# Attention outputs stored by quads and read back with the 16 rows of a head outermost, in a fused attention and mixer kernel

## The chip, the cores and the metric

The kernel runs on one core of one Trainium2 chip. The metric is the device time of one execution in microseconds (us). Beside the runs there is one profiled execution, from which every row of the profile comes. Engines are named as the profile names them: PE multiplies matrices (PEld is its weight load), DVE, ACT and POOL work on tiles, and SP issues the DMA transfers; SPq is SP's queue of instructions. Lines of the profile carry L43 nearly everywhere, because every instruction is issued through one helper at line 43; the tile names tell the groups apart.

## The reference

All is float32. One input `x` of 2048 tokens by 512 channels goes through a layer norm; the result feeds two branches, and a gate joins them.

```python
xn = layernorm(x)
# A: attention, 32 heads of 16 channels, each query sees the 256 latest keys
q, k, v = split_heads(xn @ wqkv)
s = merge_heads(softmax(mask(q @ k.T * 16 ** -0.5)) @ v) @ wo
# B: a second layer norm, 512 -> 1792 -> 512
g = silu(gelu(layernorm(xn) @ w1 + b1) @ w2 + b2)
out = x + s * g
```

## The kernel before

**Stages.** Four stages follow one another on PE: the layer norm and first projections; attention; then the two-layer branch B in four chunks of 512 tokens (`c` from 0 to 3), where each chunk ends with the product of its attention outputs with `wo` and the gate (`end_chunk`, line 953). A product of two float32 operands is made from high and low parts in three passes (`PASSES`), with the split into `hi` and `lo` done by ACT and DVE.

**Attention.** The 32 heads are handled in 8 quads of four heads (`n`). A quad has 16 blocks of 128 queries (`qb`), and each block is one slot `t = 16 n + qb` of a plan written out by hand: the loop at lines 826 to 858 issues each slot's score, probability and value products and, between them, fill work, in a fixed order. `at(t, ...)` puts a step inside slot t, `behind(t, ...)` at its end. `pv_step` (line 577) gives the unnormalised outputs of one block: head j of the quad lies in partitions 32 j to 32 j + 16, sixteen output rows and, as the seventeenth, the sum of the probabilities. ACT or DVE copies them to the tile `oraw` (printed `outs[0]`), and after four blocks one DMA of 256 KB writes `oraw` to `oT_d` in memory (line 597). There are 32 such stores.

**How the outputs come back.** `oT_d` has four groups `g` of eight heads, quads 2 g and 2 g + 1. `fetch_sums` (line 881) loads all sums into `den`; DVE takes their inverses in chunk 0, at steps 4 and 5 of the chunk's loop, and one DMA writes them to `rden_d` (line 1149). `load_o` (line 916) then brings, for a chunk and a group, the 128 output rows (`raw`, in the trace `or<-oT_d`) and beside them the inverse sums, each repeated over its head's 16 rows (`rec`, in the trace `w<-rden_d`). Both are 256 KB. In both the order of partitions is head by head, with 16 rows inside. DVE multiplies them, `split_o` splits the product into `ohl`, and `end_chunk` multiplies it by `wos`, the rows of `wo` in the same order. `wo` is brought in that order by the host, copied within memory by `stage_in` (line 638) during attention, and loaded by `fetch`.

**Order around the change.** On PE, DVE, ACT and POOL the program order is kept. On SP it is kept during attention and in chunks 0 and 1 (`nc.sync.on`); elsewhere the framework orders the issues. In chunk 0, step 5 issues the write of `rden_d`, then four pairs of `raw` and `rec` loads, and then sixteen loads of 64 KB into `xnT` (`fetch_y`, line 909), four for each of four parts `kt`, with short runs of 128 bytes; these hold the transposed inputs of chunk 1. Step 12 splits part 0 (ACT makes `yh<-xnT`, DVE the low part), and step 13 starts with ACT's `gh`, which PE needs for its next product. The ACT part of that split therefore stands ahead of the last `gh` of the chunk.

Of the kernel before, what the change touches and what calls it, by code (L numbers as in the profile page):

```python
# [9 lines left out]
F32 = mybir.dt.float32  # L10
# [7 lines left out]
S, D, H, DH, WIN, F = 2048, 512, 32, 16, 256, 1792  # L18
P = 128
NCH = S // 512  # L20
# [3 lines left out]
NQ = H // 4  # L24
# [26 lines left out]
def mixer_kernel(ctx, tc, x, wqk, wv, wo, w1, b1, w2, b2, out):  # L51


    nc = SimpleNamespace(**{name: Ordered(tc, name) for name in ("tensor", "vector", "scalar", "gpsimd", "sync")})
# [5 lines left out]
    dram = ctx.enter_context(tc.tile_pool(name="dram", bufs=1, space=bass.MemoryType.DRAM))  # L60
# [16 lines left out]
    def load(pool, tag, src, name, shape=(P, 512)):  # L77
        t = pool.tile(list(shape), F32, tag=tag, name=name)
        nc.sync.dma_start(t, src)
        return t  # L80
# [95 lines left out]
    def open_slot(i):  # L176
# [3 lines left out]
    wva = bigp.tile([P, 2, KT, 256], F32R, tag="wa", name="wva")  # L180
    wqs = {}
    xn_d = dram.tile([8, P, D], F32, name="xn_d")
    oT_d = dram.tile([4, 8, 32, S], F32, name="oT_d")
    rden_d = dram.tile([4, 8, S], F32, name="rden_d")
    h_d = dram.tile([EARLY - 2, P, 512], F32, name="h_d")
    w_d = {"w1": dram.tile([P, NF * 512], F32, name="w1_d"), "w2": dram.tile([P, NF * 512], F32, name="w2_d"),
           "wo": dram.tile([P, 4 * 512], F32, name="wo_d")}
# [387 lines left out]
    outs = {}  # L575

    def pv_step(n, qb):

        lo = max(qb - 2, 0)
        for kb in range(lo, qb + 1):  # L580
            for j in range(4):
                nc.tensor.matmul(otb[32 * j: 32 * j + DH + 1], vt[:, kb, (4 * n + j) % 16],
                                 pts[n, kb, j // 2][:, j % 2, P * (qb - kb): P * (qb - kb + 1)],
                                 start=(kb == lo), stop=(kb == qb),
                                 skip_group_check=True, tile_position=(0, 32 * j))
        if qb % 4 == 0:
            outs[0] = sgp.tile([P, 512], F32, tag="or", name=f"oraw_{n}_{qb}", bufs=2)
        t = 16 * n + qb + 1
        by = nc.vector.tensor_copy if t in ends_pair else nc.scalar.copy
        outs["copy"] = by(outs[0][:, P * (qb % 4): P * (qb % 4 + 1)], otb)  # L590
        last = outs["second" if t in ends_pair else "copy"]
        old = t - 3
        if old >= 0:
            for w in writers[old // 16, old % 16, 0] + writers[old // 16, old % 16, 1]:
                tc.add_manual_dep(last.ins, w.ins.name, ORDER, reason="the next slot writes in its place")
        if qb % 4 == 3:
            (at if n or qb > 7 else behind)(16 * n + qb + 2, nc.sync.dma_start, oT_d[n // 2, n % 2::2, :, P * (qb - 3): P * (qb + 1)], outs[0])


    mlp = {}  # L600
# [37 lines left out]
    def stage_in(kind, k):  # L638

        sl = slice(1024 * k, 1024 * (k + 1))  # L640
        nc.sync.dma_start(w_d[kind][:, sl], {"w1": w1, "w2": w2, "wo": wo}[kind][:, sl])

    def fetch(kind, f):

# [66 lines left out]
    n, raw = raws["qk"]  # L711
# [60 lines left out]
    for k, (kind, j) in enumerate([*(("w1", j) for j in range(7)), *(("w2", j) for j in range(7)), ("wo", 0), ("wo", 1)]):  # L772
        behind(23 + 4 * k, stage_in, kind, j)
# [52 lines left out]
    for t in range(-16, end + 1):  # L826
# [25 lines left out]
        if t >= 1:  # L852
            pv_step((t - 1) // 16, (t - 1) % 16)
# [27 lines left out]
    def fetch_sums():  # L881
        den = t2.tile([P, 512], F32, tag="t2", name="den")
        for g in range(4):
            nc.sync.dma_start(den[32 * g: 32 * g + 32], oT_d[g, :, DH].rearrange("a (c t) -> a c t", c=NCH))
        return den

    mlp["y"] = [load(mlp["yp"], "y", xn_d[4 + i], f"y_1_{i}") for i in range(4)]
    for f in range(6, NF, 2):
        t = gp.tile([P, 2, 512], F32, tag="ohl", name=f"hr_{f}", bufs=4)
        nc.sync.dma_start(t, h_d[f - 6: f - 4].rearrange("f p t -> p f t"))  # L890
        ready.update({f: t[:, 0], f + 1: t[:, 1]})
        if f == 8:
            den = fetch_sums()
# [22 lines left out]
    def load_o(c, g):  # L916

        cols = slice(512 * c, 512 * (c + 1))
        pool, tag = (t2, "t2") if c else (mlp["yp"], "y")
        raw = load(pool, tag, oT_d[g, :, 0:DH, cols], f"or_{c}_{g}")  # L920
        rec = mlp["w2", g // 2][:, 512 * (14 + g % 2): 512 * (15 + g % 2)].bitcast(F32)
        nc.sync.dma_start(rec, bass.AP(tensor=rden_d.tensor, offset=rden_d.offset + 8 * g * S + 512 * c,
                                       ap=[[S, 8], [0, DH], [1, 512]]))
        return raw, rec

    def split_o(c, g, raw):
# [169 lines left out]
    for c in range(2):  # L1096
# [24 lines left out]
        for i in range(NF + 1):  # L1121
# [16 lines left out]
            if c == 0:  # L1138
                if i == 3:
                    mlp["ln"] = layernorm(mlp["y"], "C1", True)  # L1140
                    y_steps(0, 5)
                if i == 4:
                    y_steps(5, 10)
                    turn_y(1, range(4))
                if i in (4, 5):
                    for j in (2 * i - 8, 2 * i - 7):
                        nc.vector.reciprocal(den[:, P * j: P * (j + 1)], den[:, P * j: P * (j + 1)])
                if i == 5:
                    nc.sync.dma_start(rden_d.rearrange("g a (c t) -> (g a c) t", c=NCH), den)
                    wanted += [load_o(0, g) for g in range(4)]  # L1150
                    for kt in range(KT):
                        fetch_y(1, kt, mlp["yy"][1][kt].bitcast(F32))
                for kt in {12: (0,), 13: (1,), 14: (2, 3)}.get(i, ()):
                    split(mlp["yy"][0][kt], mlp["yy"][1][kt], mlp["yy"][1][kt].bitcast(F32))
            else:
                steps2(i)
# [5 lines left out]
            if c and 0 <= k < 4:  # L1162
                wanted.append(load_o(c, k))
# [35 lines left out]
    for g in range(NG + 1):  # L1199
        if g < NG:  # L1200
            if g + 1 < NG:
                fetch_pair(g + 1)
            if g > NG - 3:
                raws_o = [load_o(2, 2 * (g - NG + 2) + k) for k in range(2)]
# [89 lines left out]
    for i in range(NF):  # L1294
# [9 lines left out]
        if 5 <= i < 9:  # L1304
            raw, rec = wanted
# [37 lines left out]
```

## Time and profile before

| quantity | value |
|---|---|
| median of 3 runs (all runs) | 741.33 us (741.27, 741.33, 744.54) |
| profiled execution, own time | 742.66 us |
| its span, first to last instruction | 740.9 us |
| mean granted TensorE clock | 0.998 |
| PE busy | 724.8 us, 98% of the span |
| DVE, ACT, POOL busy | 509.9, 444.0, 297.8 us |
| stores `oT_d<-oraw` | 32 of 256 KB |
| loads `or<-oT_d` and `w<-rden_d` | 16 each, of 256 KB |

The profile's page gives busy times, the chain of work that ended last, and the costliest groups. Other views of the same execution are used too: busy time by stretches (with the granted clock, the busy share of the 16 DMA engines and what they moved), the instructions of one engine in order of time, and the sums of waits. Busy time of PE includes the pipelined end of each product, so PE counted as busy can still be held for a fraction of a microsecond.

### The profile page before, as it was taken

What the parts mean: (1) busy time and instruction counts of PE and PEld (TensorE: products, weight loads), DVE (VectorE), ACT (ScalarE), POOL (GpSimd) and SP (SyncE); (2) the same over time, 40 slices, a digit from 0 to 9 for tenths busy, and PEclk for the clock granted to TensorE, in tenths of its full rate; (3) what the DMA queues carried; (4) which work ended last, traced back from release to release, by engine and by line L of the source; (5) the groups of instructions that cost most, each with busy time, mean ns of one, the idle gap of its engine ahead of it and who ended that gap; (6) DMA issues with size and microseconds to landing.
All of it is one profiled execution on the core that took longest, in us unless ns stands there. A gap on an engine that the chain in (4) does not pass through costs nothing.

```text
span 740.9 us, 18755 instructions
## 1 busy us (share of the span) xinstructions
PE 724.8 (98%) x7360; PEld 586.4 (79%) x7360; DVE 509.9 (69%) x790; ACT 444.0 (60%) x744; POOL 297.8 (40%) x644
## 2 busy tenths in 40 slices
PE   8999999999999999999999999999999999999997
PEld 7886777777778888777776688788888888888886
DVE  6886676867766778887772677656667855667643
ACT  7757777877777676788877766443644734542001
POOL 7413767867666555767877600120102000001102
PEclk9999999999999999999999999999999999999999
DMA  8633355766556535647724485746453322263611
GB/s 291 193 70 78 83 142 150 193 173 191 150 142 155 145 89 143 165 115 187 206 83 156 129 288 185 186 137 203 110 109 106 106 80 79 65 184 117 213 56 57
DMA packets 84025, 105.71 MB, mean 143 GB/s; under 512 B 36640, under 2 KB 36896, under 8 KB 83936
## 3 DMA queue, kind: packets, MB, share of 16 engines
q1 hardware_dynamic: 83936, 104.50, 49.8%
q8 instruction: 58, 0.95, 0.6%
q14 instruction: 31, 0.25, 0.1%
HBM read 54.53 MB, written 32.77 MB: 118 GB/s over the span
## 4 chain that ended last, share of the span: by engine, by line
PE 86%; DMA 4%; ACT 4%; DVE 3%; SPq 1%; POOL 1%; issue 1%; DVEq 0%; ACTq 0%
PE fb L43 18%; PE acc L43 18%; PE zo L43 13%; PE p L43 9%; PE stb L43 9%; PE s L43 6%; PE h L43 6%; PE xy L43 5%; PE pv L43 3%; ACT pt L43 3%; DMA qk<-sh 1%; DMA w<-rden_d 1%; SPq L43 1%; POOL pt L43 1%; DMA qk<-qk 1%
## 5 line engine op out<-in xcount | busy, mean ns | idle before, releaser
L43 POOL TENSOR_SCALAR_AFFINE_SELECT pt<-pt 128x256 f32<-128x256 f32 x480 | 193.1, 426 | 128.8 <-ACT pt L43 124.9
L43 ACT ACTIVATE pt<-stb 128x768 f32<-128x768 f32 (+1 forms) x244 | 188.6, 773 | 52.7 <-PE stb L43 46.3
L43 DVE TENSOR_REDUCE mt<-xy 128x4 f32<-128x1024 f32 (+1 forms) x128 | 152.6, 1192 | 4.4
L43 DVE COPY_PREDICATED xy<-upper,zo 128x512 f32<-128x512 int32 x112 | 77.8, 694 | 70.3 <-PE xy L43 63.7
L43 POOL TENSOR_TENSOR xo<-xo,gated 128x512 f32<-128x512 f32 x15 | 19.9, 1330 | 237.3 <-DVE gated L43 195.5
L43 PE MATMUL fb<-xnT,wqb 64*128 64x512 f32 (+1 forms) x684 | 104.6, 397 | 0.0
L43 PE MATMUL zo<-pt,vt 128*17 128x128 f32 x2880 | 103.7, 275 | 0.3 <-POOL pt L43 0.3
L43 PE MATMUL stb<-qk 64*128 64x384 f32 (+1 forms) x488 | 94.9, 383 | 6.1 <-ACT pt L43 4.3
L43 PE MATMUL acc<-w,gh 128*128 128x512 f32 x320 | 98.6, 389 | 0.7 <-ACT gh L43 0.7
L43 PEld LDWEIGHTS stb<-qk 64*128 64x128 f32 x488 | 45.9, 183 | 48.4 <-ACT pt L43 41.6
L43 PEld LDWEIGHTS zo<-pt,vt 128*17 128x17 f32 x2880 | 67.5, 97 | 15.7 <-issue 5.0
L43 PEld LDWEIGHTS fb<-xnT,wqb 64*128 64x128 f32 (+1 forms) x684 | 64.9, 185 | 9.3 <-issue 0.6
L43 PEld LDWEIGHTS acc<-w,gh 128*128 128x128 f32 x320 | 60.0, 188 | 13.5 <-ACT gh L43 1.2
L43 PE MATMUL acc<-w,gl 128*128 128x512 f32 x160 | 62.4, 390 | 1.0 <-DVE gl L43 1.0
L43 PE MATMUL xy<-qk 64*128 64x256 f32 (+2 forms) x536 | 58.4, 291 | 0.2 <-DVE mt L43 0.2
L43 PEld LDWEIGHTS xy<-qk 64*128 64x128 f32 x536 | 46.6, 185 | 6.7 <-issue 3.0
L43 ACT COPY oraw<-zo 128x128 f32<-128x128 f32 x108 | 28.7, 266 | 30.9 <-PE zo L43 18.8
L43 PE MATMUL s<-wos,ohl 128*128 128x512 f32 (+1 forms) x204 | 44.3, 376 | 0.0
L43 ACT ACTIVATE gated<-acc 128x512 f32<-128x512 f32 x16 | 8.7, 595 | 59.3 <-DVE acc L43 59.3
L43 PEld LDWEIGHTS s<-wos,ohl 128*128 128x128 f32 x204 | 36.8, 188 | 7.1
L43 ACT COPY p<-p 128x512 f32<-128x512 f32 x21 | 12.3, 584 | 48.6 <-PE p L43 41.4
L43 PEld LDWEIGHTS zo<-qk 64*128 64x128 f32 x448 | 37.6, 185 | 4.7 <-DVE xy L43 1.9
(190 smaller groups left out, 1237.7 us busy)
## 6 DMA issues: line engine op xcount, KB each, us to landing
qk<-sh SPq DMA_DIRECT2D x128, 128.0 KB
qk<-pjr SPq DMA_DIRECT2D x64, 128.0 KB
oT_d<-oraw SPq DMA_DIRECT2D x32, 256.0 KB
w_d<-in_w_dram SPq DMA_DIRECT2D x14, 512.0 KB
x<-in_x_dram SPq DMA_DIRECT2D x16, 256.0 KB
or<-oT_d SPq DMA_DIRECT2D x16, 256.0 KB
w<-rden_d SPq DMA_DIRECT2D x16, 256.0 KB
xo<-in_x_dram SPq DMA_DIRECT2D x16, 256.0 KB
```

The lines of the kernel that those rows point to most:

```text
L43: r = issue(*args, **kwargs)
```

## The change

The tensor `oT_d` gets the shape quads, heads of the quad, rows, tokens. A store now writes 128 rows at one constant distance, where it wrote four heads that lay two apart. Both loads of `load_o` walk their rows with the row of a head as the outer loop (16) and the eight heads as the inner one, so partition p holds row p // 8 of head p % 8 of the group; before it was head p // 16, row p % 16. The rows of `wo` have to stand in that order too: `stage_in` makes two DMAs from each of its two for `wo`, one for each quad of a group. In `fetch_sums` only the way in which the memory is addressed is changed.

```diff
-    oT_d = dram.tile([4, 8, 32, S], F32, name="oT_d")
+    oT_d = dram.tile([NQ, 4, 32, S], F32, name="oT_d")
...
-            (at if n or qb > 7 else behind)(16 * n + qb + 2, nc.sync.dma_start, oT_d[n // 2, n % 2::2, :, P * (qb - 3): P * (qb + 1)], outs[0])
+            cols = slice(P * (qb - 3), P * (qb + 1))
+            (at if n or qb > 7 else behind)(16 * n + qb + 2, nc.sync.dma_start,
+                                            oT_d[n, :, :, cols].rearrange("j r t -> (j r) t"), outs[0])
...
-        nc.sync.dma_start(w_d[kind][:, sl], {"w1": w1, "w2": w2, "wo": wo}[kind][:, sl])
+        dst, src = w_d[kind][:, sl], {"w1": w1, "w2": w2, "wo": wo}[kind][:, sl]
+        if kind == "wo":
+            for i in range(2):
+                nc.sync.dma_start(dst.rearrange("(r i j) f -> i r j f", i=2, j=4)[i],
+                                  src.rearrange("(j i r) f -> i r j f", i=2, j=4)[i])
+        else:
+            nc.sync.dma_start(dst, src)
...
-            nc.sync.dma_start(den[32 * g: 32 * g + 32], oT_d[g, :, DH].rearrange("a (c t) -> a c t", c=NCH))
+            nc.sync.dma_start(den[32 * g: 32 * g + 32],
+                              oT_d[2 * g: 2 * g + 2, :, DH].rearrange("i j (c t) -> (i j) c t", c=NCH))
...
-        raw = load(pool, tag, oT_d[g, :, 0:DH, cols], f"or_{c}_{g}")
+        raw = load(pool, tag, oT_d[2 * g: 2 * g + 2, :, 0:DH, cols].rearrange("i j r t -> r (i j) t"), f"or_{c}_{g}")
...
-                                       ap=[[S, 8], [0, DH], [1, 512]]))
+                                       ap=[[0, DH], [S, 8], [1, 512]]))
```

## The prediction

> **What bounds the kernel now.** I read the page first, then the busy time by stretches, and last, in the one stretch that matters, the chain and the engines' instructions in order of time.
>
> ```profile
> PE 724.8 (98%) x7360; PEld 586.4 (79%) x7360; DVE 509.9 (69%) x790; ACT 444.0 (60%) x744; POOL 297.8 (40%) x644
> ...
> PE 86%; DMA 4%; ACT 4%; DVE 3%; SPq 1%; POOL 1%; issue 1%; DVEq 0%; ACTq 0%
> ```
>
> The first row is busy time by engine, the second the chain that ended last. PE carries both, so a faster transfer can only gain where PE stands still: 740.9 - 724.8 = 16.1 us in all. The stretches say where (columns: length, then busy time of PE, PEld, DVE, ACT, POOL, with instructions in brackets; granted clock, DMA share, GB/s).
>
> ```profile
> 0.00:14.00 14.00, 10.87 (x59) 9.36 (x60) 10.15 (x28) 10.79 (x15) 10.31 (x18) 1.00 0.86 303
> ...
> 140.00:200.00 60.00, 58.92 (x926) 46.17 (x916) 44.42 (x56) 44.71 (x78) 40.78 (x96) 1.00 0.66 178
> ...
> 405.00:428.00 23.00, 22.72 (x323) 16.32 (x316) 13.08 (x21) 15.70 (x29) 13.58 (x27) 1.00 0.41 121
> ...
> 450.00:460.00 10.00, 10.00 (x46) 8.29 (x45) 6.14 (x11) 6.23 (x11) 0.00 (x0) 1.00 0.49 153
> ...
> 468.00:474.00 6.00, 4.28 (x18) 2.90 (x17) 5.25 (x9) 2.75 (x5) 0.00 (x0) 1.00 0.77 117
> ...
> 490.00:550.00 60.00, 60.00 (x266) 49.67 (x266) 38.22 (x79) 29.57 (x48) 4.49 (x4) 1.00 0.56 147
> ...
> 725.00:741.00 16.00, 11.51 (x63) 9.82 (x61) 5.08 (x9) 1.50 (x3) 3.86 (x3) 0.93 0.17 66
> ```
>
> PE lacks 14.00 - 10.87 = 3.13 us at the start and 740.9 - 725.0 - 11.51 = 4.4 us at the end, which the change doesn't touch, 1.72 us in 468 to 474 us, and nothing in 450 to 460 or 490 to 550; nor does the view show any in the other stretches from 428 to 725 us. What is left, 16.1 - 3.1 - 4.4 - 1.7 = 6.9 us, lies in attention, and there it waits for ACT:
>
> ```profile
> PE stb L43 <- ACT pt L43: 4.3, 17, 0.4
> ...
> ACT oraw L43 <- DMA qk<-pjr: 0.8, 3, 0.3
> ```
>
> (Sums of waits: us, times, longest.) DMA hardly holds anyone there. So the place is 468 to 474 us, the end of chunk 0. First the chain through it, then PE and ACT in order of time (start, us, engine, operation, and in brackets the idle time before and who ended it):
>
> ```profile
> 449.03 1.99 DMA rden_d<-den
> 451.03 6.73 DMA w<-rden_d
> 457.78 1.91 SPq L43
> 459.73 3.26 SPq L43
> 463.04 4.51 DMA xnT<-z_d
> ...
> 473.88 10.88 PE s L43 x48
> ```
> ```profile
> 469.60 0.73 PE L43 MATMUL acc<-w,gh 128*128 128x512 f32 x2 [0.73 <-ACT gh L43]
> 471.32 0.50 PE L43 MATMUL acc<-w,gl 128*128 128x512 f32 x1 [0.99 <-DVE gl L43]
> ```
> ```profile
> 463.28 0.62 ACT L43 CAST gh<-g 128x512 fp32r<-128x512 f32 x1 [1.47 <-issue]
> 467.65 0.62 ACT L43 CAST yh<-xnT 128x512 fp32r<-128x512 f32 x1 [3.75 <-DMA xnT<-z_d]
> ```
>
> Backwards: PE waits 0.73 + 0.99 = 1.72 us for the last `gh` and `gl` of the chunk, ACT makes that `gh` only after `yh`, and `yh` waits 3.75 us for part 0 of `xnT`, whose loads stand in SP's queue behind the eight loads of outputs and inverse sums.
>
> **The change part by part.** *The eight loads of chunk 0.* SP's instructions:
>
> ```profile
> 397.30 0.52 SPq L43 DMA_DIRECT2D oT_d<-oraw  x1
> ...
> 437.32 0.47 SPq L43 DMA_DIRECT2D b2s<-in_b_dram  x1
> ...
> 449.44 0.61 SPq L43 DMA_DIRECT2D or<-oT_d  x1
> 451.03 0.61 SPq L43 DMA_DIRECT2D w<-rden_d  x1
> 451.74 0.57 SPq L43 DMA_DIRECT2D or<-oT_d  x1
> ...
> 453.60 1.62 SPq L43 DMA_DIRECT2D w<-rden_d  x1
> 455.27 0.67 SPq L43 DMA_DIRECT2D or<-oT_d  x1
> 455.98 0.84 SPq L43 DMA_DIRECT2D w<-rden_d  x1
> 456.91 15.40 SPq L43 DMA_DIRECT2D xnT<-z_d  x16
> ...
> 535.60 8.29 SPq L43 DMA_DIRECT2D xnT<-z_d  x16
> ```
>
> An issue takes 0.57 to 0.61 us when nothing holds it; the sixth takes 1.62 and the sixteen `xnT` issues 15.40, against 8.29 (0.52 each) for the same sixteen in chunk 1. Something downstream is full. The DMA share tells what:
>
> ```profile
> 401.00:402.00 1.00, 1.00 (x12) 0.86 (x12) 0.00 (x0) 1.00 (x3) 1.00 (x4) 1.00 0.26 102
> ...
> 437.00:438.00 1.00, 1.00 (x6) 0.84 (x5) 0.94 (x3) 0.00 (x0) 0.00 (x0) 1.00 0.88 305
> 438.00:439.00 1.00, 1.00 (x6) 0.82 (x5) 0.17 (x1) 0.20 (x1) 0.72 (x1) 1.00 0.88 272
> ...
> 456.00:457.00 1.00, 1.00 (x6) 0.83 (x5) 1.00 (x2) 0.89 (x2) 0.00 (x0) 1.00 0.46 141
> 457.00:458.00 1.00, 1.00 (x6) 0.84 (x5) 0.22 (x2) 0.16 (x1) 0.00 (x0) 1.00 0.49 180
> ```
>
> While these loads queue, the share stands at 0.46 to 0.49, eight engines of sixteen, and their outermost dimension is eight heads; four microseconds after the `oT_d` store of 397.30 us, whose outermost dimension is four heads and behind which only a small transfer of 16 KB is issued, it stands at 0.26, four of sixteen. At 437 to 439 us, where transfers with 128 rows outermost run, it is 0.88 at 272 to 305 GB/s. So I read: the outermost count sets how many engines work, and sixteen rows outermost give all of them.
>
> The Trainium skill states that as a rule ("DMA: Bandwidth & Descriptors", section "Why a DMA increments its semaphore by 16 and not by 1"): a copy runs on the largest number of engines up to 16 that divides the slowest dimension of both sides. By that rule stores go from 4 to 16 and loads from 8 to 16, and the sum is the one below; by the rows alone 16 isn't shown for a count of sixteen, and the sum could stay at nothing. The trace agrees for 4 and 8 (0.26, 0.49).
>
> The new times: the write of `rden_d` at 449.03 us follows DVE's inverses, which PE's pace sets, so it and the first two issues stay. Unheld, the loads after 451.03 take seven issues at 0.64 us with gaps (451.03 to 451.74 is 0.71, then 0.62), ending at about 455.5 instead of 456.9. The seven last loads are 7 x 0.262 = 1.84 MB; at 305 GB/s, the best stretch quoted, 6.0 us, so landed by about 457.7. The first four `xnT` issues end at 455.5 + 4 x 0.52 = 457.6; their 0.26 MB at 117/0.77 = 152 GB/s (the 468 to 474 row, mostly these short runs) take 1.7 us: about 459.4. To that comes the fixed part of a transfer, 1.1 us by the write of `rden_d` (1.99 us less 0.262 MB at 305 GB/s, 0.86): 460.5. ACT is free for `yh` at 463.28 + 0.62 = 463.9. The part is there 3.4 us before it is needed, so ACT's 3.75 us and PE's 1.72 us go. Next late: the other twelve `xnT` loads, 0.79 MB, 5.2 us, land by about 465.7; they are needed only behind the last `gh`, and the product with `wo` that started at 473.9 starts near 472.1. Gain 1.72 us; it can't be more here, because PE has no other idle time between 428 and 725 us. Bounds: 0 (still eight engines) to -1.72 us.
>
> *The same loads in chunks 1 to 3*: PE 60.00 of 60.00 us in 490 to 550, and no gap until 725 us. Faster loads gain nothing; the cover is a full PE.
>
> *The 32 stores.* Each loads four engines with 64 KB; spread, 16 KB on sixteen. Transfers that share those engines land earlier. What attention could gain is bounded by the waits for DMA: ACT's largest is 0.8 us in all, quoted above. The issue may become shorter too:
>
> ```profile
> L43 SPq DMA_DIRECT2D oT_d<-oraw x32: 511/539/766, 80.4 to 425.5; - x32
> ...
> L43 SPq DMA_DIRECT2D w<-w_d x15: 319/432/507, 372.3 to 426.1; - x15
> ...
> L43 SPq DMA_DIRECT2D w_d<-in_w_dram x14: 568/590/1115, 135.0 to 278.9; - x14
> ...
> SPq L43 <- DMA oT_d<-oraw: 6.2, 4, 2.2
> ```
>
> (Minimum, median, maximum in ns.) A store now has one constant step, like `w<-w_d`: 432 instead of 539 ns, 32 x 0.107 = 3.4 us of SP's time, off PE's path. The last row is SP's own wait for a store to land; the longest, 2.2 us, holds `fetch_sums` ahead of chunk 0, where PE has no gap. I take -0.3 us for attention, near the row of DMA waits, with bounds of -2.5 us (a third of the 6.9 us that it lacks, should later transfers hold ACT unseen) and +0.7 us (a store that now lies in front of a `qk` transfer on twelve engines more, about one unspread wait).
>
> *`wo` in two pieces*: two more issues of 0.59 us on SP and the same bytes, in slots 79 and 83, with the queue's next steps 0.59 us later each. Nobody waited for DMA there by more than the row above; 0, and if the cover were gone, 1.2 us at most. *`fetch_sums`*: the same eight heads outermost and the same bytes, 0. *PE, DVE, ACT, POOL*: no instruction added or removed.
>
> **Sum**, on the profiled execution: 742.66 - 1.72 - 0.3 = 740.6 us. It was 1.33 us above the median of the runs, so against the median: 741.33 - 2.0 = 739.3; I give 739.4 us.
>
> **The rivals.** *Hidden or not spread* (no change): sixteen outermost don't give sixteen engines, or `yh` is late for another reason, the 8.29 us that SP needs for sixteen issues. Against it: part 0 needs four of them. Time 741.3 us.
>
> *More from attention*: the four engines that carry the stores also carry the small transfers, and relief ends part of the 6.9 us. For it: SP waits 6.2 us for stores. Against: PE's waits name ACT. With the bound of -2.5 us in place of -0.3 that is 741.33 - 1.72 - 2.5 = 737.1 us, just past 0.5%; it needs holds that PE's waits don't name.
>
> *Slower, by a hot address*: sixteen engines read the same 2 KB of inverse sums at once, and each walks the outputs head by head, 256 KB apart. If that cuts the rate, everything behind it in the queue is late. Four `rec` loads are 1.05 MB: 3.4 us at 305 GB/s. The slack is 3.4 us, so below 1.05/6.8 = 154 GB/s PE stops again; below 1.05/8.5 = 123 GB/s, where its 1.72 us are lost as before, the kernel gets slower. At 66 GB/s, the lowest rate of a quoted row (the last stretch, taken as the lower end), they take 15.9 us, 12.5 longer; less the slack, PE stands 9.1 us: 741.33 - 1.72 + 9.1 = 748.7 us. Against it: at 437.32 us SP issues `b2s`, a load of one row for all 128 partitions, with full engines, and the traffic stays at 272 to 305 GB/s. The Trainium skill ("DMA: Bandwidth & Descriptors", section "Latency and other measured facts") warns of rows a large power of two apart, with 207 GB/s at 512 KiB and less beyond. It would speak against the new walk of 256 KB; no run here shows that distance inside one engine, and before, the eight engines stood as far apart.
>
> **How the numbers follow.** Forecast 0.62, no change 0.18, more from attention 0.13, slower by a hot address 0.07. The forecast alone ranges from 738.2 to 740.4 us. The whole range goes from 736.6 (attention's bound, with half a microsecond for the spread of runs) to 742.0 (no change, or two issues uncovered). A difference under 0.5%, 3.7 us, is about what a measurement of this kernel can tell from no change. Faster than 737.6: the attention rival in nearly all of its cases, 0.12; slower than 745.0: 0.07; within: 0.81.
>
> **What would show it.** Right: DMA share near 0.9 between 451 and 457 us; sixteen `xnT` issues in about 8 us; no PE gap at 468 to 474; a share well above 0.26 after a lone store. Wrong: `w<-rden_d` landing later than 6.7 us after its issue, a gap of PE at another place of chunk 0 or 1, or attention's stretches longer or shorter by over 1 us.

## The result, and the profile after

The changed kernel takes 740.09 us (median of 6 runs, 739.79 to 740.39). The kernel before was measured again beside it: 743.34 us over its 6 runs (741.27 to 744.54). The ratio is 0.9962, with a 95% interval of 0.9945 to 0.9979: 0.38% faster, inside the 0.5% that the prediction called the same. By these medians the gain is 3.25 us. Beside the experiments the kernel before was run 58 more times, in two sets of 29 with medians of 742.42 and 742.32 us, and by those the gain is nearer 2.3 us. The profiled execution took 740.08 us, 2.58 us less than the one of before, with a span of 738.4 us.

Busy time by engine and the chain that ended last, of the changed kernel:

```profile
PE 725.1 (98%) x7360; PEld 587.2 (80%) x7360; DVE 509.8 (69%) x790; ACT 444.0 (60%) x744; POOL 297.6 (40%) x644
...
PE 91%; ACT 4%; DVE 2%; POOL 1%; DMA 1%; issue 1%; SPq 0%; DVEq 0%; ACTq 0%
```

PE's work is the same; DMA fell from 4% of the chain to 1% and SP's queue from 1% to 0%. The two stretches in question, with the columns as before:

```profile
450.00:460.00 10.00, 10.00 (x46) 8.29 (x45) 6.13 (x11) 6.05 (x11) 0.00 (x0) 1.00 0.86 209
...
468.00:474.00 6.00, 6.00 (x29) 4.95 (x28) 4.03 (x7) 2.88 (x4) 0.00 (x0) 1.00 0.84 220
```

While the eight loads of chunk 0 run, the DMA share is 0.86 where it was 0.49, and PE is full in 468 to 474 us, where it had 4.28 us of 6. The chain through this place no longer leaves PE, and on ACT the split of part 0 of `xnT` waits for nothing:

```profile
441.49 29.92 PE acc L43 x132
471.41 10.88 PE s L43 x48
```
```profile
463.10 0.62 ACT L43 CAST gh<-g 128x512 fp32r<-128x512 f32 x1 [1.47 <-issue]
463.63 0.62 ACT L43 CAST yh<-xnT 128x512 fp32r<-128x512 f32 x1
```

So PE's wait is gone in the way that was forecast. To follow it through all executions I use one stretch of PE's instructions, from the first `acc` product of chunk 0 to the first `h` product of chunk 1. Before:

```profile
427.90 2.43 PE L43 MATMUL acc<-w,g_first 128*128 128x512 f32 x10
...
484.60 0.39 PE L43 MATMUL h<-yh,xnT 128*128 128x512 f32 x1
```

and after:

```profile
427.73 2.65 PE L43 MATMUL acc<-w,g_first 128*128 128x512 f32 x11
...
482.12 0.39 PE L43 MATMUL h<-yh,xnT 128*128 128x512 f32 x1
```

That is 56.70 us before and 54.39 us after: 2.31 us of the 2.58 us between the two profiled executions. Of the rest, 0.17 us lies ahead of the stretch.

SP's queue, though, is not as quick as forecast:

```profile
454.64 0.60 SPq L43 DMA_DIRECT2D w<-rden_d  x1
455.34 13.92 SPq L43 DMA_DIRECT2D xnT<-z_d  x16
469.36 1.86 SPq L43 DMA_DIRECT2D y<-in_x_dram  x4
```

The eight loads are issued unheld (0.55 to 0.60 us each), but the sixteen `xnT` issues still take 13.92 us, not 8.3.

The trace also records when a load is complete: each `xnT` load ends with the last of sixteen updates of its semaphore. For the fourth load of part 0 that is at 467.55 us in the kernel before, 0.10 us ahead of `yh`; in the changed kernel it is at 463.50 us, 0.13 us ahead of `yh`. Part 0 now comes just in time, with next to nothing of the 3.4 us of slack that was forecast.

Of the other signs that the prediction named, the DMA share in 451 to 457 us is 0.91, and a lone store reaches 0.66. Of the four loads `w<-rden_d`, the last two land 7.07 and 8.05 us after their issue, over the 6.7 us that it named as a sign of being wrong.

### The profile page after: what moved, and what is told of

Read it like the earlier page. It is cut to its first block, busy times and chain, and to the rows that moved or that the text cites. A ratio compares the mean times of both kernels' runs of the same rounds, so it can differ in the third digit from the quotient of the medians.

```text
span 738.4 us, 18757 instructions
## 1 busy us (share of the span) xinstructions
PE 725.1 (98%) x7360; PEld 587.2 (80%) x7360; DVE 509.8 (69%) x790; ACT 444.0 (60%) x744; POOL 297.6 (40%) x644
## 4 chain that ended last, share of the span: by engine, by line
PE 91%; ACT 4%; DVE 2%; POOL 1%; DMA 1%; issue 1%; SPq 0%; DVEq 0%; ACTq 0%
PE acc L43 21%; PE fb L43 19%; PE zo L43 13%; PE stb L43 9%; PE p L43 9%; PE s L43 6%; PE h L43 6%; PE xy L43 5%; ACT pt L43 4%; PE pv L43 3%; POOL pt L43 1%; DVE xy L43 1%; DMA x<-in_x_dram 1%; DVE mt L43 0%; PE tr L43 0%
## 5 line engine op out<-in xcount | busy, mean ns | idle before, releaser
L43 PEld LDWEIGHTS stb<-qk 64*128 64x128 f32 x488 | 45.8, 183 | 48.3 <-ACT pt L43 41.4
```

What stands on the lines that cost most here:

```text
L43: r = issue(*args, **kwargs)
```

## The experiments

### The loads alone, and the stores alone

The first kernel has the new order in the loads and in `wo`'s rows, on the old tensor and with the old stores:

```diff
-        raw = load(pool, tag, oT_d[g, :, 0:DH, cols], f"or_{c}_{g}")
+        raw = load(pool, tag, oT_d[g, :, 0:DH, cols].rearrange("a r t -> r a t"), f"or_{c}_{g}")
...
-                                       ap=[[S, 8], [0, DH], [1, 512]]))
+                                       ap=[[0, DH], [S, 8], [1, 512]]))
```

> The kernel before with the loads of raw outputs and inverse sums (and wo's rows) in the new order, 16 rows outermost; the stores stay as before, four heads outermost. Theory: the gain is the end of chunk 0's wait for part 0 of xnT, and it comes from the loads. Then the stretch from the first acc product of chunk 0 to the first product with wo is 43.5 us, as in the changed kernel (before: 428.06 to 473.88, 45.8), and the time equals the changed kernel's within 0.3 us. Rival: the stores on four engines made the queue late; then the stretch stays at 45.8 us and the time stays that of before.

The second has the new tensor and stores, with the loads by heads:

```diff
-        raw = load(pool, tag, oT_d[2 * g: 2 * g + 2, :, 0:DH, cols].rearrange("i j r t -> r (i j) t"), f"or_{c}_{g}")
+        raw = load(pool, tag, oT_d[2 * g: 2 * g + 2, :, 0:DH, cols].rearrange("i j r t -> (i j) r t"), f"or_{c}_{g}")
...
-                                       ap=[[0, DH], [S, 8], [1, 512]]))
+                                       ap=[[S, 8], [0, DH], [1, 512]]))
```

> The changed kernel with the loads put back to eight heads outermost (wo's rows back in that order, still in two pieces); only the stores are new. Theory: stretch of chunk 0 45.8 us, time as before within 0.5 us; a lone store still takes 1 us at a DMA share of 0.6 or more instead of 4 us at 0.2, and attention ends within 0.2 us of where it ended before. Rival: stretch 43.5 us and the whole gain.

The loads alone: 740.15 us, ratio to before 0.9959 (0.9944 to 0.9974; the medians, 740.15 and 742.42 us, give 0.9969), the stretch to the first `h` is 54.40 us (43.52 to the first product with `wo`, the milestone of the expectation). That is the whole gain. The stores alone: 742.17 us, ratio 0.9993 (0.9980 to 1.0006), stretch 56.18 us (45.30 by the expectation's milestone, where 45.8 was expected, and within what the kernel before shows from execution to execution, see below); `yh` waits again:

```profile
466.98 0.62 ACT L43 CAST yh<-xnT 128x512 fp32r<-128x512 f32 x1 [3.19 <-DMA xnT<-z_d]
```

The stores did become faster. Busy time by stretches after a store that stands alone, first the kernel before (issued at 415.33 us), then the kernel with the new stores alone (issued at 415.22 us):

```profile
416.00:417.00 1.00, 1.00 (x28) 0.57 (x24) 0.00 (x0) 0.94 (x2) 1.00 (x4) 1.00 0.20 25
417.00:418.00 1.00, 1.00 (x17) 0.81 (x11) 0.00 (x0) 0.65 (x2) 1.00 (x4) 1.00 0.17 10
418.00:419.00 1.00, 1.00 (x20) 0.63 (x20) 0.00 (x0) 0.71 (x2) 0.67 (x3) 1.00 0.24 70
419.00:420.00 1.00, 1.00 (x26) 0.74 (x20) 0.00 (x0) 0.33 (x2) 0.39 (x1) 1.00 0.34 119
```
```profile
416.00:417.00 1.00, 1.00 (x30) 0.61 (x26) 0.00 (x0) 0.82 (x2) 1.00 (x4) 1.00 0.70 262
417.00:418.00 1.00, 1.00 (x15) 0.89 (x13) 0.00 (x0) 0.77 (x2) 1.00 (x4) 1.00 0.00 0
```

Four microseconds at 0.17 to 0.34 became one at 0.70, and SP's own waits for stores, 6.2 us before, are gone from its list. The updates of the semaphores agree: this store has one update 0.93 us after its issue and four more up to 421.17 us, 5.84 us after it, in the kernel before; with the new stores it has sixteen, the last at 417.25 us, 2.03 us after its issue. For each load `or<-oT_d` and `w<-rden_d` it is one and eight before, and sixteen in the changed kernel. PE's path shows nothing of the quicker stores: the stretch in chunk 0 starts at 427.79 us here, at 428.18 with the loads alone and old stores, and between 427.78 and 428.08 in five executions of the kernel before.

### The split behind the last `gh`

All transfers as before; only the place of ACT's split of part 0 moves.

```diff
-                for kt in {12: (0,), 13: (1,), 14: (2, 3)}.get(i, ()):
+                for kt in {13: (0, 1), 14: (2, 3)}.get(i, ()):
```

> The kernel before, all transfers unchanged, but the split of part 0 of xnT stands at step 13 of chunk 0, behind the chunk's last gh, instead of step 12. Theory: only ACT's order made PE wait, so PE's 0.73 and 0.99 us waits go, the stretch is 43.5 to 43.9 us and the time as the changed kernel's within 0.5 us. Rival: the late transfers themselves are needed (the last ohl or the next inputs), the wait moves to the product with wo, and the stretch stays above 45 us.

742.14 us, ratio 0.9993 (0.9981 to 1.0004), stretch 56.18 us to the first `h`. By the milestone of the expectation, the first product with `wo`, it is 43.52 us, as its theory had it, but the time is not the changed kernel's: the wait has moved behind that milestone, into the product with `wo`, where the rival put it. PE's waits for `gh` and `gl` are gone, and in their place stands one in the product with `wo` (sums of waits of PE, 440 to 490 us):

```profile
PE s L43 <- DVE gated L43: 1.5, 1, 1.5
```

Its chain shows why:

```profile
471.92 2.15 DMA xnT<-z_d
474.22 0.63 ACT xnT L43
474.88 0.69 DVE xnT L43
475.57 0.62 DVE acc L43
...
478.15 0.69 DVE gated L43
478.88 5.74 PE s L43 x24
```

The last part of `xnT` lands, is split by ACT and DVE, and only behind that DVE does the additions and the gate that free a bank for the product. So the queue had two deadlines, part 0 for the last `gh` and part 3 for the gate, and a new order of instructions meets only the first. In the changed kernel both parts come sooner: part 3's copy on ACT starts at 470.92 us instead of 474.19 in the kernel before.

### The same kernel before, four more times

> The kernel before, unchanged, in another execution: runs of it lay between 741.3 and 744.5 us where those of the changed kernel lie within 0.6 us. Theory: the spread is the length of the wait in chunk 0, so time less that stretch is 696.8 us, as in the first execution (742.66 - 45.82), within 0.4 us, whatever the time. Rival: the spread comes from the start or from attention, and the stretch is 45.8 us at any time.

> The kernel before, unchanged, for one more execution with a profile. Theory: if it is over 743.5 us, the stretch of chunk 0 (first acc product to the first h product of chunk 1, 56.70 us in the first execution) is longer by the difference. Rival: it is 56.7 us and the difference lies before or behind.

> The kernel before, unchanged, a third execution with a profile. Theory: over 743.5 us only with a stretch of chunk 0 longer by the difference. Rival: the stretch is 56.7 us at any time.

> The kernel before, unchanged, a fourth execution with a profile. Theory: over 743.5 us only with a stretch of chunk 0 longer by the difference. Rival: the stretch is 56.7 us at any time.

The profiled execution of the first took 742.85 us with the stretch at 56.67 us; to the first product with `wo` it is 45.78, and 742.85 - 45.78 = 697.1 us agrees with the expectation, but so near to the first execution it told nothing. The other three did not reach 743.5 us, but they differ enough. ACT's wait for part 0 in the longest and in the shortest of them:

```profile
468.13 0.62 ACT L43 CAST yh<-xnT 128x512 fp32r<-128x512 f32 x1 [4.33 <-DMA xnT<-z_d]
```
```profile
466.47 0.62 ACT L43 CAST yh<-xnT 128x512 fp32r<-128x512 f32 x1 [2.62 <-DMA xnT<-z_d]
```

| execution | time, us | `yh` after the first `acc`, us | stretch to first `h`, us | time less stretch, us |
|---|---|---|---|---|
| before | 742.66 | 39.75 | 56.70 | 685.96 |
| before, 2nd (before_again) | 742.85 | 39.72 | 56.67 | 686.18 |
| before, 3rd (before_b) | 743.15 | 40.34 | 57.28 | 685.87 |
| before, 4th (before_c) | 741.49 | 38.62 | 55.56 | 685.93 |
| before, 5th (before_d) | 742.05 | 39.14 | 56.19 | 685.86 |
| stores alone | 741.92 | 39.19 | 56.18 | 685.74 |
| loads alone | 740.66 | 36.96 | 54.40 | 686.26 |
| changed | 740.08 | 35.90 | 54.39 | 685.69 |

Over five executions of one program the time ranges over 1.66 us and the stretch over 1.72 us, while what is left stays within 0.32 us. So the spread in these five is the length of this wait, and so is the gain of the change. The longest runs have no profile, and it is not shown that they are the same wait, only longer. Of the 58 runs beside the experiments nine lie above 743.5 us, and eight of these nine have a mean granted clock of 0.997, where the other 49 have 0.998 to 1.000; whether the lower clock is a cause or comes of a longer wait stays open. The programs without the wait spread by 0.6 us (changed) and 0.8 us (loads alone).

The table gives PE's reserve too. `yh` starts 35.90 us after the first `acc` when it needn't wait, yet at 36.96 PE lost nothing; at 38.62 it lost 55.56 - 54.39 = 1.17 us, at 40.34 it lost 2.89 us. The loss is the start less 37.45 us: PE bears about 1.5 us of ACT's wait.

### One kind of load alone

The amount of work stays the same in these two kernels. The first keeps the sums by heads:

```diff
-                                       ap=[[0, DH], [S, 8], [1, 512]]))
+                                       ap=[[S, 8], [0, DH], [1, 512]]))
```

> The changed kernel with only the inverse sums read head by head again (eight heads outermost), so that each output row is multiplied by another head's inverse sum; that mismatch is the part of the computation left out. Theory: both loads weigh alike, a half of the spreading brings the queue forward by half, and from the first acc product of chunk 0 to the first h product of chunk 1 it takes 54.4 to 55.2 us (54.40 in the changed kernel, 56.70 before). Rival, a hot address: reading the outputs with 16 engines is the quick part, so this one shows the whole gain, 54.4 us, and rec_only is later by over 0.5 us.

The second keeps the outputs by heads:

```diff
-        raw = load(pool, tag, oT_d[2 * g: 2 * g + 2, :, 0:DH, cols].rearrange("i j r t -> r (i j) t"), f"or_{c}_{g}")
+        raw = load(pool, tag, oT_d[2 * g: 2 * g + 2, :, 0:DH, cols].rearrange("i j r t -> (i j) r t"), f"or_{c}_{g}")
```

> The changed kernel with only the outputs read head by head again, the inverse sums with 16 rows outermost, again with mismatched sums. Theory: 54.4 to 55.2 us over the same stretch, as raw_only. Rival, a hot address (sixteen engines reading the same 2 KB at once): the loads of inverse sums need more packet time for their bytes than before, and the stretch is over 0.5 us longer than in raw_only.

Beside them the kernel before took 742.32 us. Outputs spread: 740.35 us, stretch 54.40 us, all of the gain. Sums spread: 740.71 us, stretch 54.86 us, four fifths of it. `yh` starts 36.53 us after the first `acc` in the one and 37.89 in the other, past PE's reserve by 0.4 us. The difference of the stretches, 0.46 us in one execution each, is just under the 0.5 us that the rival asked for, and the ratios of the times overlap (0.9962 to 0.9983 and 0.9968 to 0.9988). This pair alone leaves it open whether one address is hot. Either load alone relieves the queue nearly enough, probably because part of its bytes then leaves the eight engines that the other still uses (with both kinds on eight, the share stood at 0.46 to 0.49).

### The reserve of the changed kernel

Copies from the input to a spare tensor are put ahead of the `xnT` loads, two in one kernel and six in the other:

```diff
                     wanted += [load_o(0, g) for g in range(4)]
+                    for e in range(2):
+                        nc.sync.dma_start(spare_d[e], x[P * e: P * e + P, :])
```

> The changed kernel with two copies of 256 KB within memory, of input rows to a spare tensor, put into SP's queue between the loads of chunk 0 and the sixteen xnT loads. Theory of the prediction: part 0 lands 3.4 us before it is needed; two copies take about 1.7 us at 305 GB/s, so nothing waits and the stretch to the first h product of chunk 1 stays at 54.4 us. Rival: the queue is later than predicted (its sixteen issues took 13.9 us instead of 8.3), the slack is under 1 us, and the stretch is 55 us or more.

> As extra2 with six copies, about 5.2 us of transfers. Theory of the prediction: 1.8 us more than the slack, so the wait comes back at the last gh of chunk 0 or in the product with wo, and the stretch is 55 to 56.5 us. Rival with a slack under 1 us: 58 us or more.

Two copies: 740.53 us, ratio to before 0.9974 (0.9965 to 0.9984), stretch 54.40 us; but on ACT part 0 comes too late:

```profile
464.54 0.62 ACT L43 CAST yh<-xnT 128x512 fp32r<-128x512 f32 x1 [0.58 <-DMA xnT<-z_d]
```

Six copies: 743.31 us, ratio 1.0011 (1.0000 to 1.0022), stretch 56.48 us, and `yh` 39.52 us after the first `acc`. By the reserve found above the loss is 39.52 - 37.45 = 2.07 us; measured 56.48 - 54.39 = 2.09. Both come out as the theory of the prediction had them at PE, but not at ACT: with a slack of 3.4 us ACT would not have waited behind two copies. What protects PE is the sum of 0.13 us of slack at ACT and PE's own 1.5 us. The rival was right that the slack is under 1 us; its 58 us for six copies left PE's reserve out.

### Sixteen engines on one address

The loads of inverse sums are replaced by loads of the same size and shape from the outputs:

```diff
-        nc.sync.dma_start(rec, bass.AP(tensor=rden_d.tensor, offset=rden_d.offset + 8 * g * S + 512 * c,
-                                       ap=[[0, DH], [S, 8], [1, 512]]))
+        nc.sync.dma_start(rec, oT_d[2 * g: 2 * g + 2, :, 0:DH, cols].rearrange("i j r t -> r (i j) t"))
```

> The changed kernel with the loads of inverse sums replaced by loads of the same size and shape from the outputs, so that sixteen engines read sixteen different rows; the division by the sums is thereby left out. In the changed kernel two loads of inverse sums that stand alone in chunk 2 (issued at 658.10 us) take from 659.4 to 662.9 us, 3.5 us for 0.52 MB, as long as on eight engines (3.1 to 3.4 us). Theory, a hot address: reading the same 2 KB from all engines holds them, and the two loads now take 1.5 to 2.2 us. Rival: runs of 2 KB or the destination set the pace, and they take 3.1 us or more.

Two such loads, 0.52 MB, stand alone in chunk 2. Busy time in half microseconds, two rows each: first the second execution of the kernel before (eight engines, eight addresses), then of the changed kernel (sixteen engines, one address at a time), then of this one (sixteen engines, sixteen addresses):

```profile
662.50:663.00 0.50, 0.50 (x4) 0.42 (x3) 0.50 (x1) 0.00 (x0) 0.00 (x0) 1.00 0.48 180
663.00:663.50 0.50, 0.50 (x4) 0.42 (x3) 0.07 (x1) 0.39 (x1) 0.00 (x0) 1.00 0.51 172
```
```profile
661.00:661.50 0.50, 0.50 (x4) 0.42 (x3) 0.40 (x1) 0.07 (x1) 0.00 (x0) 1.00 1.05 180
661.50:662.00 0.50, 0.50 (x4) 0.42 (x3) 0.45 (x2) 0.17 (x1) 0.00 (x0) 1.00 0.90 139
```
```profile
660.00:660.50 0.50, 0.50 (x4) 0.41 (x3) 0.22 (x1) 0.23 (x1) 0.00 (x0) 1.00 1.01 303
660.50:661.00 0.50, 0.50 (x4) 0.39 (x3) 0.11 (x1) 0.36 (x1) 0.00 (x0) 1.00 0.95 320
```

With different rows the packets of the two loads start from 659.2 to 661.2 us, 2.0 us; with the same rows it is 3.5 us. From the first issue to the last update of a semaphore it is 4.12 against 5.17 us. The expectation's theory holds in its number: in the rows shown, sixteen engines that read the same 2 KB move 139 to 180 GB/s at a share of 0.90 to 1.05, no more than eight engines do at half a share (172 to 180), against 303 to 320 on different rows. In the microsecond before these rows the same-row loads show 168 to 184 GB/s at 0.52 to 0.54, so the share is not full throughout. Two things stay open: different rows were measured in one execution only, and the new loads differ also in their tensor and in the distance from one row to the next (256 KB instead of 8 KB), which no run separates from the repeated row. Spreading the inverse sums made their own loads no shorter; that it still brought most of the gain fits with the outputs having their eight engines to themselves for part of the time, which is argued and not shown.

The same kernel shows what these loads cost in chunk 0:

```profile
454.21 11.83 SPq L43 DMA_DIRECT2D xnT<-z_d  x16
```
```profile
463.42 0.61 ACT L43 CAST yh<-xnT 128x512 fp32r<-128x512 f32 x1
```

Its part 0 is complete at 460.35 us, 3.07 us before ACT takes it up, where the changed kernel has 0.13 us. Of the 3.15 us between the two landings 1.13 us is the earlier issue (454.21 instead of 455.34 us: nothing waits for `rden_d` here); the remaining 2.0 us or so are what the loads of inverse sums cost the queue, an estimate from one execution of each.

## Why the prediction came out right, step by step

**The place and the cause: right.** Chunk 0's wait for part 0 of `xnT`, behind loads that used eight engines, was what held PE, as the loads alone and the five executions of the kernel before show. Outside the stretch the profiled executions of the table agree within 0.6 us.

**The size: too small.** The forecast took PE's idle rows, 0.73 + 0.99 = 1.72 us, and said that it can't be more; by the stretch it is 2.31 us. The rows understate it because a product is drawn with 0.39 us while the next one may start 0.227 us later (twelve `acc` products take 2.72 us), so that each gap hides some 0.16 us of waiting, and the few products between the gaps are drawn apart too. The right term is the time between two milestones of PE, not the sum of its idle time. The kernel before also varies by this very wait: its 741.33 us, the median of three runs from which the forecast subtracted 2.0, became 743.34 over six runs and 742.42 and 742.32 over two sets of 29. So the base was about 1 us low and the gain 0.3 us or more too small; the two errors partly cancel, and that the 740.09 measured lies only 0.7 us above the forecast's 739.4 is luck in part.

**The landing of part 0: wrong, and luckily without consequence.** The step took the seven loads at 305 GB/s and the `xnT` issues at 0.52 us: part 0 at 460.5 us. The eight loads ran at 209 GB/s in 450 to 460 us, the sixteen issues took 13.92 us, and two more copies already made ACT wait at 464.54 us. Part 0 landed at 463.50 us, 3.0 us later than forecast and 0.13 us before ACT took it up: the slack of 3.4 us was not there. That it was just in time is luck, and PE's reserve of 1.5 us behind ACT, which the step left out, would have covered for a little more. By the estimate above some 2 us of the 3.0 come from the loads of inverse sums; in the kernel with different rows part 0 landed at 460.35 us, near the forecast's 460.5, with the issue 1.13 us earlier. Its sixteen issues still take 11.83 us; why they take longer here than in chunk 1 was not tried.

**Eight to sixteen engines: right for the stores and the outputs.** A lone store went from a share of 0.17 to 0.34 up to 0.70, and the updates of its semaphore, beside the early one, from four to sixteen; those of a load went from eight to sixteen. The rule of the Trainium skill ("DMA: Bandwidth & Descriptors", section "Why a DMA increments its semaphore by 16 and not by 1") agrees with that. For the inverse sums it gives the engines and not the time: sixteen updates for each load, and 3.5 us for two of them.

**Attention, -0.3 us: not there.** With the new stores the stretch in chunk 0 starts between 427.51 and 428.38 us in seven kernels, and with the old ones between 427.78 and 428.28 us in seven executions. A gain from quicker stores does not stand out of this spread, and the rival that hoped for more from attention falls.

**`wo` in two pieces, chunks 1 to 3, `fetch_sums`: right at nothing, within half a microsecond.** The time less the stretch in chunk 0 is 685.69 us in the changed kernel and 685.86 to 686.18 us before.

**The rival of a hot address: the slow loads exist, and they cost the slack, not PE.** It set 154 GB/s as the rate for the four loads at which the slack is used up and below which PE stops again. The pair that stands alone moves 0.52 MB in 3.5 us, 150 GB/s, and of the slack 0.13 us is left. PE does not stop, because part 0 is still in time. What the prediction held against this rival did not bear on it: `b2s`, the load of one row for all partitions, is issued at 437.32 us, but in the kernel before the sixteen updates of its semaphore come from 441.58 to 443.39 us, so the rows from 437 to 439 us need not show it at all. The new walk of 256 KB within an engine, of which the Trainium skill ("DMA: Bandwidth & Descriptors", section "Latency and other measured facts") made one wary with 207 GB/s at 512 KiB (for copies within memory, with 214 GB/s as the full rate), shows no loss here: 303 to 320 GB/s, against 305 in the best stretch that the prediction quoted.

## What to carry to other kernels

Where a transfer's outermost dimension is under sixteen, look at the DMA share: here a flat 0.26 (outermost four) or 0.46 to 0.49 (outermost eight), with SP's issues growing long in the second case, was a queue on few engines, and it delayed what was queued behind it. Read the slack of a transfer from its completion in the trace and not from a rate: the 3.4 us of the forecast were 0.13 us. Price a wait by the time between two milestones of the bounding engine, and run the kernel before several times first: a wait that changes from run to run is part of the thing to be measured. Before a late transfer is moved out of the way by reordering, follow the same queue to its next deadline.

## What the runs showed of the hardware that I had not expected

Sixteen engines reading the same 2 KB at once were no faster than eight engines reading eight different rows: 0.52 MB in 3.3 to 3.5 us against 3.1 to 3.4 us; the same shape over different rows took 2.0 us in the one execution of it. The share does not tell the two apart well: it was 0.5 on eight engines and went from 0.52 to 1.05 on sixteen at 131 to 184 GB/s. A load that repeats a row can therefore use all sixteen engines and still take as long as on eight.
